# Attention in 64x64 quadrants of TensorE on blocks of 256 rows, two rows on a partition, with a planner that orders the jobs of all engines

## The chip, the cores and the metric

One core of one Trainium2 chip. The metric is the device time of one execution in microseconds (us); a kernel is run several times in turn with the kernel before on the same chip, and the median and the range are given. A run is called slow when it is over 1.5% above the fastest run of the same kernel, otherwise fast; ratios use fast runs only. Engines: PE is TensorE (PEld its weight loads), DVE is VectorE, ACT is ScalarE, POOL is GpSimd, SP is SyncE, whose queue issues nearly all transfers here.

## The reference

A retention layer (attention without a softmax, with a decay between positions) and then a gated MLP. Eight sequences of 576 rows, 8 heads of 64, all inputs fp32.

```python
scores = scale * np.matmul(q, k.transpose(0, 1, 3, 2))
gamma = 1.0 - 2.0 ** (-5.0 - np.arange(H))
Dmat = np.where(rel >= 0, gamma[:, None, None] ** rel[None], 0.0)   # rel = row - column
x = np.matmul(scores * Dmat, v)                 # heads side by side: [8, 576, 512]
h = gelu_tanh(x @ w_in)                         # [.., 1024]
u, v = h[..., :512], h[..., 512:]
v_n = (v - mean) / sqrt(var + 1e-6) * g_ln
v_s = np.einsum('ts,bsd->btd', w_sg, v_n) + b_sg[None, :, None]   # mixes the 576 rows of a sequence
out = x + (u * v_s) @ w_out
```

Since the decay is a product of a factor of the row and one of the column, the kernel multiplies q and v by powers of gamma, works in blocks of rows, and carries the sum of k times v of earlier blocks as a state.

## The kernel before

Two sequences make 9 tiles of 128 rows. A tile is loaded with one row on a partition, so that each contiguous run of a transfer is 64 fp32 values, 256 bytes. Attention uses the whole array for the transposes, half of its rows for the scores, half of its columns for the tile's own part of the output, and the whole array, with a block-diagonal state that is half zeros, for the state's part.

```python
def load(i):
    ...
            nc.sync.dma_start(t[p0:p0 + n, :, :], src[2 * p + b, :, r0:r0 + n, :].transpose([1, 0, 2]))

def attn_T(i):      # 8 transposes of 128x128
    ...
            nc.tensor.transpose(tp[:, a, kk, :], f[:, a, kk * 128:(kk + 1) * 128], ident[:])

def attn_S(i):      # 8 matmuls on half of the rows
    ...
            nc.tensor.matmul(sc[:, hh, kk, :], s["qkT"][r, 1, kk, :], s["qkT"][r, 0, kk, :], ...)

def attn_O(i, evac):
    ...
            nc.tensor.matmul(ot[:, kk, :n], st["zbd"][:, kk, :], s["qkT"][:, 0, kk, :n], ...)      # state
    ...
            nc.tensor.matmul(ot[64 * hh:64 * hh + 64, kk, :], s["vb"][:, 2 * kk + hh, :], s["ret"][:, hh, kk, :], ...)
```

The weights: w_in is loaded in quarters, each one transfer over 128 partitions, `moe_w_in.rearrange("(c p) f -> p c f", p=128)`. The order of everything is written out in one loop over the tiles, which also deals out units of gating (`mlp_W`) and final projection (`mlp_O`) between the attention steps. Gating mixes all rows of a sequence, so none can start before the first 576 rows, w_sg and its transposes are through.

## Time and profile before

| | before |
|---|---|
| median of 4 runs | 249.22 us (249.12 to 250.46) |
| profiled span | 248.1 us |
| TensorE busy | 220.2 us, 89% |
| packets under 512 bytes | 113,824 of 120,606 |

A table of stretches of the kernel before. The columns are: the stretch in us, its length, busy us (and instructions) of PE, PEld, DVE, ACT and POOL, the granted TensorE clock, the mean busy share of the DMA engines, and GB/s.

```profile
0.00:20.00 20.00, 12.98 (x133) 6.46 (x134) 16.95 (x37) 5.97 (x9) 11.49 (x26) 0.93 1.03 235
20.00:60.00 40.00, 32.25 (x397) 24.39 (x401) 22.77 (x40) 23.75 (x44) 25.13 (x41) 0.91 0.96 197
140.00:220.00 80.00, 76.17 (x906) 53.74 (x919) 46.33 (x77) 50.28 (x95) 49.20 (x81) 1.00 0.73 163
```

Up to 60 us the DMA engines are full (shares of 1.03 and 0.96) and TensorE has holes; from 140 on TensorE is busy 95% and the DMA engines 73%.

Busy time hides how much of TensorE is really used, because matmuls overlap in the pipeline: in this kernel a 128-column matmul is shown as 219 ns and the next one starts 56 ns after it. So I use one more measure below, **lost TensorE time** up to a moment. Every matmul group has a weight load in the trace, and those records are complete (144 loads for the gating input `hv`, of whose 144 matmuls the trace before holds 126). I give each the step at which its matmuls follow one another when nothing holds them (the steps of the prediction: 216 ns for 512 columns, 122 for 288, 56 for 128 and half of that for half of the array; for quadrants 8 for 64 columns, 14 for 128, and 16 in the state update, where I take two to run together; 0 for filler matmuls), sum the steps of all loads issued by that moment, and subtract the sum from the moment. It contains idle time, fillers, changes of the array's shape, drains, and time at a lower granted clock. The 14 and the 16 are estimates, a quarter of 56 and twice 8. In the changed kernel forty quadrant matmuls of 128 columns start within 123.79 to 124.38 us, 15 ns each, and the sixteen of a state update take 120.85 - 120.49 = 0.36 us with a change of shape of 0.10 behind them, 16 ns each. The absolute value leans on these steps; differences between kernels with the same matmuls don't. The clock's part is at most the length of a stretch times what the granted clock lacks to 1: by 60 us up to 5.0 us in the kernel before (0.93 and 0.91 in the table), 1.6 in the changed kernel, 3.6 in its second trace. So differences of 2 or 3 us in the lost time of two traces can be the clock's.

### The profile page before, as it was taken

The page shows a single profiled execution, that of the slowest core. Times are in us where ns is not written, and L with a number is a line of the kernel's source. Part 1 is how long each engine was busy: PE and PEld are TensorE (multiplying, and loading weights), DVE is VectorE, ACT ScalarE, POOL GpSimd, SP SyncE. Part 2 cuts the span into 40 slices and gives each one's busy share as a digit, 9 for nine tenths or more (in the row PEclk, how much of TensorE's full clock was granted, in tenths as well). Part 3 has the DMA queues.
Part 4 walks back from the last instruction along what each step waited for, and adds up shares of the span by engine and source line. Part 5 has one row for each costly group of instructions (what it writes and reads, how often), then busy time and mean ns, then how long its engine had stood idle before and what let it go on. Part 6 is the DMA issues. An engine that isn't in the chain of part 4 may idle for free.

```text
span 248.1 us, 6439 instructions
## 1 busy us (share of the span) xinstructions
PE 220.2 (89%) x2543; PEld 154.0 (62%) x2580; DVE 141.4 (57%) x251; ACT 141.7 (57%) x258; POOL 137.3 (55%) x237
## 2 busy tenths in 40 slices
PE   7737749889998999989998999899989999899893
PEld 2415547677655776666666776577657766676561
DVE  8984636747645665556646764476537554564240
ACT  2334566844665656756574667756565657755512
POOL 4387948652674776656655656555646766441100
PEclk9988997979999999999999999999999999999999
DMA  7999999693677985892898965993879778201314
GB/s 151 284 281 221 225 239 232 142 189 68 142 177 203 206 174 122 234 230 49 186 229 182 215 151 152 223 203 81 193 199 211 167 171 184 74 3 42 128 45 169
DMA packets 120606, 42.02 MB, mean 169 GB/s; under 512 B 113824, under 2 KB 114424, under 8 KB 120576
## 3 DMA queue, kind: packets, MB, share of 16 engines
q1 hardware_dynamic: 119376, 40.93, 72.7%
q0 software_dynamic: 656, 0.66, 1.7%
q8 instruction: 20, 0.33, 0.6%
q10 hardware_dynamic: 544, 0.02, 0.1%
q14 instruction: 10, 0.08, 0.1%
HBM read 32.80 MB, written 9.44 MB: 170 GB/s over the span
## 4 chain that ended last, share of the span: by engine, by line
PE 71%; POOL 4%; ACT 3%; issue 3%; DVE 2%; DMA 1%; ACTq 0%; POOLq 0%; DVEq 0%
PE wp L339 14%; PE hu L327 11%; PE op L355 11%; PE hv L289 11%; PE tp L221 6%; PE ot L254 4%; PE sc L233 3%; PE op L352 3%; PE zp L275 3%; PE ot L250 2%; ACT vn L317 1%; POOL qkb L200 1%; POOL vb L200 1%; PE wtp L192 1%; ACT vmid L314 1%
## 5 line engine op out<-in xcount | busy, mean ns | idle before, releaser
L237 DVE TENSOR_TENSOR ret<-sc,tri 128x1024 bf16<-128x1024 f32 x32 | 39.0, 1220 | 28.3 <-PE sc L233 28.3
L343 DVE TENSOR_TENSOR gT<-wp,uT 128x288 bf16<-128x288 f32 x64 | 29.3, 457 | 41.8 <-PE wp L339 41.7
L302 POOL TENSOR_SCALAR rs<-mv 128x1 f32<-128x1 f32 x36 | 8.0, 223 | 78.9 <-DVE mv L300 50.4
L339 PE MATMUL wp<-wT,vn 128*128 128x288 bf16 x256 | 42.7, 289 | 3.7 <-ACT vn L317 3.7
L200 POOL TENSOR_TENSOR qkb<-qf,gqv 128x512 bf16<-128x512 f32 x36 | 37.6, 1044 | 5.1 <-DMA qf<-in_q_dram 4.9
L292 ACT ACTIVATE vg<-hv 128x512 f32<-128x512 f32 x36 | 21.5, 597 | 32.5 <-issue 18.4
L327 PE MATMUL hu<-xT,w_in 128*128 128x128 bf16 x576 | 39.4, 223 | 0.0
L200 POOL TENSOR_TENSOR vb<-vf,gqv 128x512 bf16<-128x512 f32 x36 | 37.4, 1038 | 3.5 <-DMA vf<-in_v_dram 3.5
L330 ACT ACTIVATE uT<-hu 128x512 bf16<-128x512 f32 x36 | 21.5, 597 | 28.6 <-PE hu L327 28.6
L289 PE MATMUL hv<-w_in,xT 128*128 128x512 bf16 x126 | 36.4, 390 | 1.5 <-issue 0.6
L327 PEld LDWEIGHTS <-w_in 128*128 128x128 bf16 x576 | 35.0, 100 | 0.3
L355 PE MATMUL op<-w_out,gT 128*128 128x512 bf16 x126 | 33.1, 379 | 0.9
L339 PEld LDWEIGHTS <-vn 128*128 128x128 bf16 x256 | 24.3, 98 | 12.7 <-ACT vn L317 5.0
L358 ACT ACTIVATE ob<-op 128x512 f32<-128x512 f32 x36 | 21.4, 594 | 18.8 <-PE op L355 18.5
L298 DVE BATCH_NORM_STATS2 bst<-vg 128x6 f32<-128x512 f32 x36 | 24.8, 688 | 11.9 <-ACT vg L292 11.9
L223 DVE COPY qkT<-tp 128x1024 bf16<-128x1024 bf16 x36 | 24.1, 669 | 7.7 <-PE tp L221 7.7
L221 PE MATMUL tp<-ident,qkb 128*128 128x128 bf16 x288 | 23.8, 227 | 3.4 <-POOL qkb L200 2.5
L258 ACT ACTIVATE xT<-ot 128x512 bf16<-128x512 f32 x36 | 21.2, 590 | 8.6 <-PE ot L254 8.1
L317 ACT ACTIVATE vn<-vg,nm,rs 128x512 bf16<-128x512 f32 x32 | 25.8, 805 | 0.1
L221 PEld LDWEIGHTS <-qkb 128*128 128x128 bf16 x288 | 17.1, 101 | 8.3 <-POOL qkb L200 3.4
L339 PE MATMUL wp<-wT,vmid 128*128 128x288 bf16 x64 | 18.5, 289 | 4.2 <-ACT vmid L314 2.7
L303 POOL TENSOR_TENSOR rs<-rs,mhalf 128x1 f32<-128x1 f32 x36 | 20.4, 567 | 3.0
(72 smaller groups left out, 275.3 us busy)
## 6 DMA issues: line engine op xcount, KB each, us to landing
out_dram<-ob SPq DMA_DIRECT2D x36, 256.0 KB, 2.2
qf<-in_q_dram SPq DMA_DIRECT2D x32, 256.0 KB, 4.1
kf<-in_k_dram SPq DMA_DIRECT2D x32, 256.0 KB, 4.7
vf<-in_v_dram SPq DMA_DIRECT2D x32, 256.0 KB, 4.7
wst<-in_moe_w_in_dram SPq DMA_DIRECT2D x4, 512.0 KB, 5.5
qf<-in_q_dram SPq DMA_DIRECT2D x8, 128.0 KB, 3.3
kf<-in_k_dram SPq DMA_DIRECT2D x8, 128.0 KB, 3.4
vf<-in_v_dram SPq DMA_DIRECT2D x8, 128.0 KB
```

Source lines behind the costliest of these rows:

```text
L200: nc.gpsimd.tensor_tensor(out_[:], in_[:], gqv[:, a, m, :].unsqueeze(2).to_broadcast([128, H, D]), op=Alu.mult)
L221: nc.tensor.transpose(tp[:, a, kk, :], f[:, a, kk * 128:(kk + 1) * 128], ident[:])
L223: nc.vector.tensor_copy(qkT[:], tp[:])
L237: nc.vector.tensor_tensor(ret[:].rearrange("p a k t -> p (a k) t"), sc[:].rearrange("p a k t -> p (a k) t"), msk[:].unsqueeze(1).to_broadc ...
L289: nc.tensor.matmul(hv[:], xTs[p][:, kk, 128 * m:128 * m + 128], w_in[:, kk, F2:], start=(kk == 0), stop=(kk == KK - 1))
L292: nc.scalar.activation(vg[:], hv[:], Act.Gelu_apprx_tanh)
L298: nc.vector.bn_stats(bst[:], vg[:])
L317: nc.scalar.activation(vn[:], vg[:], Act.Identity, scale=rs[:], bias=nm[:])
L327: nc.tensor.matmul(hu[:, c, :], w_in[:, kk, 128 * c:128 * c + 128], xTs[p][:, kk, 128 * m:128 * m + 128], start=(kk == 0), stop=(kk == KK ...
L339: nc.tensor.matmul(ps[:], vns[t0 + j][e][:, 128 * c:128 * c + 128], wT[e][j][:, half * HS:(half + 1) * HS], start=(j == 0), stop=(j == SB ...
L343: nc.vector.tensor_tensor(gTs[p][:, c, col:col + HS], ps[:], uTs[p][:, c, col:col + HS], op=Alu.mult)
L355: nc.tensor.matmul(op[:], gTs[p][:, c, r], w_out[:, c, :], start=False, stop=(c == KK - 1), skip_group_check=True)
```

## The change

The intent: TensorE bounds the kernel, so attention goes to 64x64 quadrants, four matmuls at a time, without the half-empty state. Blocks grow to 256 rows with two neighbouring rows on a partition, so the runs of a transfer are 512 bytes. The handwritten order is replaced by a planner that, while the program is built, simulates all engines with assumed durations and lays down the order in which each engine's jobs then run. Its assumptions for a transfer are in `place`. The diff, cut to its core:

```diff
+class Planner:
+    def place(self, j, t):
+        j.start = t
+        if j.nbytes:
+            self.free[j.eng] = t + j.dur
+            per = (8.0 + 0.0325 * j.run) * j.nbytes / j.run / 16.0
+            self.dma_free = max(self.dma_free, t + 1300.0) + per + 100.0
+            j.out = self.dma_free + 700.0
+            self.dmas.append(j.out)
...
-    def load(i):
-                nc.sync.dma_start(t[p0:p0 + n, :, :], src[2 * p + b, :, r0:r0 + n, :].transpose([1, 0, 2]))
+    def a_load(b, t):
+        f_ = new("ld", [128, H, 2 * D], F32)
+        if ns == 2:
+            nc.sync.dma_start(f_[:], src[2 * p + e, :, r0:r0 + 256, :].rearrange("h (p s) d -> p h (s d)", s=2))
+        else:      # the 64 rows at the end of one sequence and the 64 at the start of the next
+            for c, (e, r0) in enumerate(ch):
+                nc.sync.dma_start(f_[64 * c:64 * c + 64, :, :D], src[2 * p + e, :, r0:r0 + 64, :].rearrange("h p d -> p h d"))
...
-            nc.sync.dma_start(wst[:], moe_w_in.rearrange("(c p) f -> p c f", p=128)[:, c:c + 2, half * F2:(half + 1) * F2])
+            w4 = moe_w_in.rearrange("(a c h d) f -> a c d h f", a=2, c=2, h=2)
+            for cc in range(2):
+                nc.sync.dma_start(wst[half, c][64 * cc:64 * cc + 64], w4[c, cc, :, :, half * F2:(half + 1) * F2])
...
+    def a_T(b):
+                            R, C = slice(64 * r, 64 * r + 64), slice(64 * c, 64 * c + 64)
+                            nc.tensor.transpose(tpf[C, r, o:o + 64], qkb[R, s, a, 2 * kk + c, :], ident[R, R])
...
+    def a_OS(b, g):              # output of block b, with the last scores of block b + 1 in it
+        a_O(b, st.pop((b, "zs")))
+        a_S(b + 1, g)            # (not for the first two blocks and the last one)
+        nc.tensor.drain()
+        a_O2(b)                  # the half of the state part whose quadrants write the other bank
...
+    FREE = 1                     # up to this block the scores stay outside the output step
+    pl.plan()
```

The MLP's matmuls are the same; only their order is the planner's.

## The prediction

> **What bounds the kernel now.** I read the page first, then the groups, the timeline of one steady block, and last a table of stretches.
>
> ```profile
> PE 220.2 (89%) x2543; PEld 154.0 (62%) x2580; DVE 141.4 (57%) x251; ACT 141.7 (57%) x258; POOL 137.3 (55%) x237
> ...
> PE   7737749889998999989998999899989999899893
> ...
> PEclk9988997979999999999999999999999999999999
> DMA  7999999693677985892898965993879778201314
> ```
>
> TensorE (PE) is the busiest engine by far; the others are near 57%. The first nine slices (6.2 us each) look different from the rest: PE has holes while DMA stands at 9. So there are two regimes. The starts of the score matmuls (line 233) bound the stretches of the next table: the first scores start at 8.43 us, those of block 7 at 56.81, those of the last block at 223.50. Its columns are length, busy us (and count) of PE, PEld, DVE, ACT and POOL, granted clock, DMA share, GB/s.
>
> ```profile
> 0.00:8.43 8.43, 6.40 (x37) 2.88 (x38) 7.17 (x24) 2.23 (x3) 3.69 (x13) 1.00 0.84 205
> 8.43:56.81 48.38, 35.69 (x454) 25.82 (x461) 29.79 (x49) 25.93 (x46) 32.92 (x53) 0.89 1.05 219
> 56.81:223.50 166.69, 158.58 (x1883) 112.37 (x1911) 97.02 (x164) 103.25 (x192) 98.60 (x165) 1.00 0.73 164
> 223.50:248.10 24.60, 19.58 (x173) 12.90 (x174) 7.44 (x15) 10.23 (x17) 2.08 (x6) 1.00 0.25 97
> ```
>
> In the head the DMA engines are full (1.05) and the clock drops to 0.89; in the long middle PE is busy 158.6 of 166.7 us at full clock. Busy is not throughput, so I took steps from one start to the next:
>
> ```profile
> 119.06 0.62 PE L221 MATMUL tp<-ident,qkb 128*128 128x128 bf16 x8
> 119.52 1.06 PE L327 MATMUL hu<-xT,w_in 128*128 128x128 bf16 x16
> 120.41 0.65 PE L339 MATMUL wp<-wT,vn 128*128 128x288 bf16 x4
> 120.90 0.29 PE L339 MATMUL wp<-wT,vmid 128*128 128x288 bf16 x1
> 121.02 0.39 PE L352 MATMUL op<-ident,xT 128*128 128x128 bf16 x4
> 121.46 0.81 PE L355 MATMUL op<-w_out,gT 128*128 128x512 bf16 x3
> 122.21 0.40 PE L233 MATMUL sc<-qkT 64*128 64x128 bf16 x8
> 122.54 1.04 PE L289 MATMUL hv<-w_in,xT 128*128 128x512 bf16 x4
> ```
>
> The first column is the start. Sixteen 128-column matmuls take 120.41-119.52 = 0.89 us, 56 ns each; the five of 288 columns take 122 ns each. A 512-column one steps by 216 ns in the single records. Eight half-array score matmuls run in pairs, 4 x 56 = 0.22 us, yet the next full-array one starts 0.33 us after them: changing the array's shape costs about 0.1 us (93 ns in the records). The kernel's own warm-up already has quadrant matmuls (64 x 64 weights, 64 columns):
>
> ```profile
> 8.76 0.45 PE L409 MATMUL scr<-warm 64*64 64x64 bf16 x32
> ```
>
> One lasts 193 ns, so the last starts at about 9.01: 31 steps in 0.25 us, 8 ns each, four in 32 ns.
>
> By these steps, with counts from the program (some records are missing in the trace), PE's work is 190 us: MLP and its weights 144.2, attention 46.0 (transposes 288 x 56 = 16.1; scores 288 x 28 = 8.0; state part of the output 6.8; own part 288 x 28 = 8.0; state update 128 x 56 = 7.1). With 4 shape changes per 128-row block, 144 x 0.093 = 13.4. What is left of the span is idle: 8.4 before the first scores, 20 in blocks 0 to 6, 10 in the 28 blocks of the middle (0.35 each), 5 in the last stretch, and 2 of filler matmuls. The middle is bound by PE's issue, the head by loads.
>
> [...] The changed kernel does that with a drain and a semaphore in every output step. The old kernel has no such step, so its trace can't price it.
> - [...] a 128-column matmul is shown as 219 ns but steps by 56.
> - [...] The page has 113,824 of 120,606 packets under 512 B; the median record of a 256 B packet is 18 ns, of a 2048 B one 84 ns.
>
> **The change part by part.** I counted instructions in the compiled order of both kernels.
> - *Transposes:* 288 full ones become 1152 of 64x64. 1152 x 7.9 ns = 9.1 us against 16.1: -7.0.
> - *Scores:* 512 x 128 columns and 64 x 64 columns in quadrants: 512 x 14 + 64 x 7.9 = 7.7 against 8.0: -0.4. Mask and chunk stay at 128 rows.
> - *State update:* 480 of 64 columns, but a chunk's rows lie in one half of the array, so only two run together: 480 x 15.8 = 7.6 against 7.1: +0.4.
> - *Output, both parts:* 224+512 of 128 columns and 32+64 of 64: 736 x 14 + 96 x 7.9 = 11.0 against 14.8: -3.8. The old one multiplied by a block-diagonal state that was half zeros.
> - Attention sum: 35.4 against 46.0, **-10.7 us**.
> - *Shape changes:* the order has 106 against 145: 39 x 0.093 = **-3.6**.
> - *Drain:* 20 output steps wait for the scores ahead of them to leave the array. A matmul shows 0.22 us and steps by 0.056, so an estimate is 0.2 us each: **+4**.
> - *Loads:* two rows on a partition make runs of 512 B. Interpolating between 18 and 84 ns gives some 27 ns per 512 B packet, an estimate, so 299 against 227 GB/s. By 57 us some 9.4 MB of q, k, v are loaded: 31.5 instead of 41.5 us of a full queue, **-10** in the head. In the middle loads are hidden either way.
> - *First block:* twice as big, and POOL now also casts k that ACT cast before; its first scores come later, by some 2 us of the same head: **+2**, partly covered by the planner's first-projection-before-second-block order.
> - *Order:* PE jobs are chosen by earliest start and due time; in the middle I give it a third of the 10 us: **-3**. The tail is the same chain (last projection, statistics, norm, gating, output): 0. Fillers run in gaps: 67 instead of 18, nothing on the path. The MLP has the same matmuls.
> - VectorE copies the same transpose and mask volume in bigger pieces, ScalarE evacuates the same xT and state; both fall or stay, about 140 us of work each, so neither binds at 220.
>
> Sum: -10.7-3.6+4-10+2-3 = -21. With rounding to whole stalls that I can't place, 249 - 21 = 228, or counted forward: 179.5 (work) + 9.9 (106 changes) + 4 + 18 (head) + 7 + 5 + 1 (time over span) = 224. I take the forward sum, because the order of the head is new as a whole.
>
> **Rivals.**
> 1. *Evacuation becomes the wait.* Transposes, scores and output now share two PSUM buffers of two banks each, and a copy of 2048 transposed elements takes twice the 669 ns of now. For: every output step needs both buffers free at once. Against: a 256-row block holds them for some 8 us of 2 x 10.5. If it bites, 0.5 us for each of 20 blocks: 234.
> 2. *A plan that the chip doesn't keep.* The order is fixed from assumed durations; each engine runs strictly in that order, so one late job holds those behind it. For: the head depends on landings, which the trace shows at 4 to 5.5 us with wide variation. Against: POOL, DVE and ACT have 40% slack. It would cost 5 to 15 us: up to 240.
> 3. *The planner is much better than I allow.* If head stalls fall to 10 and middle stalls to 3, 211.
> 4. *Loads were hidden anyway.* Then the head's holes are dependences (fewer matmuls exist before the first gating) and the 10 us don't come: 234. The two in 8.43:56.81 can't be told apart without a run.
>
> **Range and chances.** 224 us; a range of 211 to 238 holds rivals 3 and 1 or 4. To stay within 2% (above 244), the drain and the plan must eat the whole saving in matmuls and loads; I give that 0.06, and slower 0.03.
>
> **What would show it.** Right: transposes stepping by 8 ns; a score group to a projection about 0.1 us beyond its own steps; q, k, v packets of 512 B near 27 ns; block 3's scores (row 640 on) before 40 us; a steady 256-row block in 10.4 to 10.8 us against 11.9 now. Wrong: quadrant steps above 12 ns, PE waiting for VectorE or ScalarE in most blocks, a drain of over 0.5 us, or PE idle in the head as now.

## The result, and the profile after

| | before | after |
|---|---|---|
| median | 249.22 us | 241.47 us (239.23 to 242.31, 4 runs) |
| profiled span | 248.1 us | 239.6 us |
| ratio | | 0.968 (95% interval 0.961 to 0.975) |
| the same kernel again (e1) | 249.00 us | 239.78 us, ratio 0.965 (0.958 to 0.971) |

A ratio is the mean time of one kernel's fast runs over that of the other's in the same rounds, so it is not quite the ratio of the medians. The change is faster by 3.2% by the ratio. I had predicted 224 us with a range of 211 to 238: the direction was right, the size was less than half of what I said, and 241.5 is outside the range.

The page of the changed kernel: busy engines, slices of 6 us each, packets, and the chain that ended last.

```profile
PE 215.4 (90%) x4440; PEld 148.0 (62%) x4485; DVE 137.1 (57%) x230; ACT 135.1 (56%) x234; POOL 126.8 (53%) x198
...
PE   7975839887989999999999999899999999999993
...
DMA  6999589999899985898564658971110220111324
GB/s 177 251 237 259 138 260 328 290 277 267 176 302 280 310 219 149 244 294 238 149 196 137 193 140 253 298 198 47 48 47 11 80 94 34 59 47 44 131 92 175
DMA packets 70765, 42.92 MB, mean 179 GB/s; under 512 B 14817, under 2 KB 63993, under 8 KB 70721
...
PE 76%; DMA 13%; issue 4%; ACT 3%; SPq 1%; POOL 1%; ACTq 0%
```

The packets are indeed bigger. From slice 11 on TensorE is at 9 nearly throughout. But the first ten slices have holes as before, and 13% of the chain that ended last is DMA, against 1% before. The same stretches as above:

```profile
0.00:20.00 20.00, 17.22 (x219) 8.26 (x223) 16.93 (x31) 4.62 (x7) 14.07 (x31) 1.00 0.99 230
20.00:60.00 40.00, 28.96 (x730) 20.39 (x737) 20.43 (x33) 23.27 (x41) 26.75 (x35) 0.96 0.96 258
140.00:220.00 80.00, 76.89 (x1588) 54.19 (x1602) 45.19 (x75) 50.38 (x89) 34.69 (x57) 1.00 0.34 104
```

The 17.22 us of PE in the first 20 are mostly fillers (55 of the head's 67, 12 us by their steps). Between 20 and 60 us TensorE is busy less than before, 29.0 against 32.3 us, although the transfers move 258 instead of 197 GB/s. In the lost TensorE time:

| lost TensorE time, us | before | after | after, second trace (e1) | predicted for after |
|---|---|---|---|---|
| 0 to 20 us | 17.1 | 18.1 | 18.1 | |
| 20 to 60 us | 15.0 | 19.1 | 18.5 | |
| together, up to 60 us | 32.1 | 37.2 | 36.6 | about 21 |
| 60 us to the end | 25.1 | 22.3 | 20.3 | about 22.5 |
| work by the steps | 190.8 | 180.1 | 180.1 | 179.5 |

The column "predicted" comes from the prediction's forward sum: 18 for the head, and of its 9.9 + 4 for shape changes and drains those that fall before 60 us (26 of 106 changes in the trace, 2.4 us, and some 5 drains, 1 us); the rest of its 44.9 us belongs after 60, less the 1 us by which a time exceeds the profiled span. The work is no test of the prediction, since it is the same counts with the same steps; that the part after 60 us came out as predicted is one. So **the whole miss of 16 to 17 us lies before 60 us**. The clock doesn't explain it: the changed kernel had the higher granted clock there (1.00 and 0.96 against 0.93 and 0.91).

Its single steps can be read from a steady stretch of the changed kernel (start, duration to the last end, engine, line, operation, count):

```profile
119.75 0.29 PE L575 MATMUL wp<-wT,vmid 128*128 128x288 bf16 x1
119.97 0.71 PE L367 MATMUL pp<-ident,qkb 64*64 64x64 bf16 x64
120.49 0.42 PE L421 MATMUL zp<-vb,qkb 64*64 64x64 bf16 x16
...
124.38 0.39 PE L393 MATMUL pp<-qkT 64*64 64x128 bf16 x12
124.88 0.24 PE L439 MATMUL pp<-qkT,zb 64*64 64x128 bf16 x2
```

The 64 quadrant transposes take 120.49 - 119.97 = 0.52 us, 8 ns each. The change of shape ahead of them is 119.97 - 119.75 - 0.12 = 0.10 us. The drain shows in the last two lines: the twelve scores need about 12 x 14 = 0.17 us, so the last starts near 124.55, and the held-back part of the output starts at 124.88: 0.3 us where I had put 0.2. The other output steps with scores in them from 60 to 205 us show the same, 0.31 to 0.33 us. All of that is close to the prediction.

What TensorE waits for in the head is found with the other engines. The waits of the changed kernel between 20 and 62 us (engine and line, what ended the wait, us in total, times, longest):

```profile
POOL qkb L350 <- DMA ld<-in_q_dram: 12.9, 3, 5.7
...
ACT wnat L295 <- DMA ld<-in_moe_w_sg_dram: 5.5, 2, 4.8
...
PE zp L421 <- ACT zb L427: 4.4, 2, 4.1
```

GpSimd, which scales q, waits three times for q to land, 12.9 us in all. ScalarE waits 4.8 us for w_sg, and behind it in its queue stands the eviction of the state for which TensorE then waits 4.1 us. The landings in the trace (some of them read from the instruction that waited for the data) against those that the plan assumes, in us: q of block 1 20.8 against 13.9, v of block 2 31 against 20.8, first part of w_sg 32.8 against 21.6, q of block 3 38 against 26, q of block 4 46.8 against 33.6. By packets, 9.42 MB had been moved by 40 us in the kernel before, and 9.23 MB in the changed one: **in the first 40 us the bigger packets brought no byte earlier.** By 60 us it is 12.65 against 14.95 MB. One gap stands out, from 24 to 30 us, just after SyncE has issued the four small transfers into the middle tile's buffers (21.7 to 24.4 us); the columns are those of the stretches above:

```profile
24.00:30.00 6.00, 5.25 (x195) 4.16 (x196) 4.21 (x5) 1.58 (x3) 3.66 (x4) 1.00 0.59 141
```

### The profile page after: what moved, and what is told of

The parts are those of the page before. It is cut to its first block, busy times and chain, and to the rows that moved or that the text cites. A ratio compares the mean times of both kernels' runs of the same rounds, so it can differ in the third digit from the quotient of the medians.

```text
span 239.6 us, 10051 instructions
## 1 busy us (share of the span) xinstructions
PE 215.4 (90%) x4440; PEld 148.0 (62%) x4485; DVE 137.1 (57%) x230; ACT 135.1 (56%) x234; POOL 126.8 (53%) x198
## 4 chain that ended last, share of the span: by engine, by line
PE 76%; DMA 13%; issue 4%; ACT 3%; SPq 1%; POOL 1%; ACTq 0%
PE wp L575 17%; PE hu L559 13%; PE op L596 13%; PE hv L517 12%; PE pp L439 7%; DMA ld<-in_q_dram 4%; PE pp L367 4%; PE pp L393 4%; PE op L593 3%; DMA ld<-in_moe_w_out_dram 3%; DMA ld<-in_moe_w_in_dram 3%; PE zp L421 3%; DMA ld<-in_moe_w_sg_dram 2%; ACT xT L506 1%; PE scr L248 1%
## 5 line engine op out<-in xcount | busy, mean ns | idle before, releaser
L403 DVE TENSOR_TENSOR ret<-pp,msk 128x1024 bf16<-128x1024 f32 x32 | 38.9, 1220 | 27.8 <-PE pp L393 27.6
L350 POOL TENSOR_TENSOR qkb<-ld,gqv 128x512 bf16<-128x512 f32 x36 | 37.1, 1051 | 15.6 <-DMA ld<-in_q_dram 12.9
L350 POOL TENSOR_TENSOR vb<-ld,gqv 128x512 bf16<-128x512 f32 x36 | 38.2, 1081 | 5.8 <-DMA ld<-in_v_dram 3.6
L582 DVE TENSOR_TENSOR gT<-wp,uT 128x288 bf16<-128x288 f32 x64 | 28.7, 453 | 21.0 <-PE wp L575 20.8
L521 ACT ACTIVATE vg<-hv 128x512 f32<-128x512 f32 x36 | 21.5, 596 | 20.3 <-PE hv L517 18.1
L372 DVE COPY qkT<-pp 128x2048 bf16<-128x2048 bf16 (+1 forms) x20 | 22.2, 1111 | 15.1 <-PE pp L367 15.1
L548 ACT ACTIVATE vn<-vg,mv 128x512 bf16<-128x512 f32 x32 | 25.0, 809 | 8.8 <-POOL mv L536 8.7
L506 ACT ACTIVATE xT<-pp 128x512 bf16<-128x512 f32 (+1 forms) x40 | 24.6, 665 | 8.2 <-PE pp L439 8.2
L575 PEld LDWEIGHTS <-vn 128*128 128x128 bf16 x256 | 23.9, 98 | 6.7
L517 PEld LDWEIGHTS <-xT 128*128 128x128 bf16 x144 | 12.6, 98 | 13.1 <-ACT xT L506 2.4
L341 POOL CAST qkb<-ld 128x1024 bf16<-128x1024 f32 (+1 forms) x20 | 19.5, 975 | 0.5 <-DMA ld<-in_k_dram 0.5
L248 PE MATMUL scr<-warm 128*128 128x512 bf16 x61 | 17.6, 436 | 2.2 <-DVE warm L221 1.2
L421 PE MATMUL zp<-vb,qkb 64*64 64x64 bf16 x480 | 13.8, 194 | 6.1 <-ACT zb L427 4.4
```

Of the source, the lines that this page charges most:

```text
L350: nc.gpsimd.tensor_tensor(dst[:, s], src[:, s], gqv[:, a, 2 * n + s, :].unsqueeze(2).to_broadcast([128, H, D]), op=Alu.mult)
L372: nc.vector.tensor_copy(st[b, "qkT"][:].rearrange("p c a k t -> p c (a k t)")[:, :, :w], st.pop((b, "tp"))[:].rearrange("p c a k s t -> p ...
L403: nc.vector.tensor_tensor(ret[:].rearrange("p r (k t) -> p (r k) t", k=2), sc[:].rearrange("p r (k t) -> p (r k) t", k=2), msk2[:].rearran ...
L506: nc.scalar.activation(dst, src, Act.Copy)
L517: nc.tensor.matmul(hv[:], xTs[p][:, kk, 128 * m:128 * m + 128], w_in[:, kk, F2:], start=(kk == 0), stop=(kk == KK - 1))
L521: nc.scalar.activation(vgs[i][:], cur.pop(("hv", i))[:], Act.Gelu_apprx_tanh)
```

## The experiments

Eighteen kernels ran, in five groups, each group on one chip with its own runs of the kernel before. The rivals for the lost head: A, the loads of w_in, now in halves of 64 partitions, are slow; B, the order is wrong because the plan's landings are; C, the bytes of q, k and v bound the head, whatever the order; D, the fused output step holds block 2 until block 3 has landed. E and F came later: queue order of one tile, and a late start of block 0.

### Which term is it

**e1, the unaltered kernel again.**

> The changed kernel unaltered, as the base on this chip: some 241.5 us, ratio to the kernel before 0.968. All theories say the same; it sets the base for the other three.

239.78 us (238.71 to 241.66), ratio 0.965. The same within the spread of this kernel, about 3 us, which is larger than that of the kernel before. Differences below 2 us are therefore read from the lost time or left open.

**e2, w_in in full-width loads.**

```diff
-            for cc in range(2):
-                nc.sync.dma_start(wst[half, c][64 * cc:64 * cc + 64], w4[c, cc, :, :, half * F2:(half + 1) * F2])
+            for hh in range(2):
+                nc.sync.dma_start(wst[half, c][:, hh, :], w4[c, :, :, hh, half * F2:(half + 1) * F2])
```

> The eight loads of the first weight matrix each fill all 128 partitions (one row of 512 columns) in place of 64 partitions with two rows; same bytes, packets, number and order. Theory A (half-partition weight loads are slow: their 2048 B packets take 144 ns against 84 in the kernel before, 1024 packets x 60 ns / 16 = 4 us of the full queue in the first 20 us): packets back to 85 to 95 ns, second block's q lands 3 to 4 us earlier, time 236 to 239. Rival (the first 20 us are bound by the memory's rate, some 250 GB/s, whatever the shape): packets of q and k get slower in exchange and the time stays within 1 us of the base.

271.06 us, ratio 1.090. A failed experiment, with something to learn. The slices of e2, 6.7 us each:

```profile
DMA  7311114659999899997985654799111012112224
GB/s 182 100 51 51 51 51 119 184 129 297 330 276 277 211 261 274 305 277 201 315 229 152 184 160 143 198 267 303 70 43 42 34 49 81 45 42 78 96 104 157
```

For four slices only 51 GB/s arrive at a DMA share of 0.1. From 10 to 36 us the queue of w_in took 13.1% of the time of the 16 engines, which is the time of 2.1 engines, an estimate by this share. Why this form of the load fills no more, no run shows. What e2 shows about the question is only this: 17.6 us more lost by 60 us became 29.6 us in the time (271.06 - 241.47), since the delay went on (25.1 us more lost by 100 us; the granted clock was 0.50 from 20 to 60 us, which is part of it). Here a late head was not made up later.

**e3, the plan with slower transfers.**

```diff
-            per = (8.0 + 0.0325 * j.run) * j.nbytes / j.run / 16.0
+            per = 1.4 * (8.0 + 0.0325 * j.run) * j.nbytes / j.run / 16.0
```

> Only the planner's own estimate of a transfer is multiplied by 1.4, so that its landings agree with the measured ones (second block's q 18.3 us in the plan against 20.8 measured; 13.9 in the plan as it was). Theory B (the order of ScalarE and TensorE in the head is made for landings that come 7 to 13 us too early, so jobs that are ready sit behind casts of weights that have not landed: ScalarE 27.9 to 32.8 us, TensorE 4.1 us behind it): the 4.1 us wait of the state update goes, 3 to 7 us gained, 235 to 238. Rival (TensorE would find nothing else to do, loads bound the head): less than 1.5 us.

242.98 us (241.35 to 243.87), ratio 0.975; lost by 60 us 39.5. A plan nearer to the real landings is not better, if anything worse (0.969 to 0.980 against 0.958 to 0.971 for e1). B in this plain form falls.

**e4, half of q, k and v (wrong result on purpose, relative error 1.27).** Four of eight heads are loaded and used twice; all compute instructions stay, and read the four heads twice.

```diff
-            nc.sync.dma_start(f_[:], src[2 * p + e, :, r0:r0 + 256, :].rearrange("h (p s) d -> p h (s d)", s=2))
+            nc.sync.dma_start(f_[:, :4], src[2 * p + e, :4, r0:r0 + 256, :].rearrange("h (p s) d -> p h (s d)", s=2))
...
```

> Wrong result on purpose: of q, k, v only four of eight heads are loaded and used twice, so half the bytes and packets of these loads with the same order, instructions and packet sizes. If loads bound the head (theory C), the 30 us of queue time of q, k, v in the first 60 us fall to 15 and the time falls by 8 to 14 us, to 228 to 234. If the head is bound by dependences, by the order or by issue of transfers, by less than 3 us.

229.00 us (228.69 to 229.48), ratio 0.921 (0.918 to 0.924): 10.8 us below e1 of the same chip. Its stretches:

```profile
0.00:20.00 20.00, 17.24 (x221) 8.18 (x224) 16.33 (x31) 5.20 (x8) 16.06 (x35) 1.00 0.88 193
20.00:60.00 40.00, 36.07 (x963) 26.30 (x972) 27.55 (x44) 29.18 (x51) 31.41 (x48) 1.00 0.69 191
```

TensorE's first 20 us stay as they were; between 20 and 60 TensorE is busy 36.1 instead of 29.0 us, while the DMA share falls to 0.69. Lost time by 60 us: 29.3 against 36.6. C is supported: half of the bytes of q, k and v cost 10.8 us, 7.3 of them in the head and some 3.5 later. Of the 7.3, up to 3.6 show up as granted clock (1.00 in e4, 0.91 between 20 and 60 us in e1). But 29 us stay lost even so, 18 of them before 20 us. The weights were loaded whole in e4, so it doesn't say what those are made of.

### The form of the loads

**e5, both halves of w_in in flight at once** (the upper halves from ScalarE's queue).

```diff
-            for cc in range(2):
-                nc.sync.dma_start(wst[half, c][64 * cc:64 * cc + 64], ...)
+            for cc, q_ in enumerate((nc.sync, nc.scalar)):
+                q_.dma_start(wst[half, c][64 * cc:64 * cc + 64], ...)
```

> The half-partition loads of the first weight matrix stay as they are, but the lower halves are issued by SyncE and the upper halves by ScalarE, so that both halves are in flight at once (the run with one row per load gave two-engine transfers and told nothing of this). Theory A (144 ns a packet comes from filling only 64 partitions at a time): packets fall to 84 to 100 ns, the weights land by 14 us in place of 17, and the time falls by 2 to 4 us from the base of 239.8. Rival (it comes from the source, or from the mixture with 512 B packets): packets stay over 130 ns, time within 1 us of the base.

240.61 us, ratio 0.965, packets still 150 ns (median of the 2048-byte packets): no help. ScalarE's four issues took until 14.5 us, and the last packet of w_in began at 21.6 us, so the time is no clean test of the form; the length of the packets is.

**e7, runs of 256 bytes again.**

```diff
-            nc.sync.dma_start(f_[:], src[...].rearrange("h (p s) d -> p h (s d)", s=2))
+            for s_ in range(2):
+                nc.sync.dma_start(f_[:, :, s_ * D:(s_ + 1) * D],
+                                  src[...].rearrange("h (p s) d -> p s h d", s=2)[:, s_])
```

> Undoes one part: every q, k, v load of a 256-row block is two transfers of 256 B runs (one per row slot) in place of one of 512 B runs; same tiles, same order. By the step of the prediction (512 B runs gave 10 us in the head) this should cost 8 to 12 us: 248 to 252, with first gating at 69 or later. Rival (the head's rate is some 250 GB/s with either, as the kernel before reached 280 to 290 GB/s with 256 B runs beside full-width weights): 1 to 4 us.

258.35 us, ratio 1.036 (1.033 to 1.039): the bigger runs are worth some 17 to 19 us in this kernel. But not where I had put them. By 60 us e7 has lost 41.6 against 37.2, only 4.4 us more; 12.7 are lost between 100 and 140 us, where the changed kernel loses 3.9 (up to 5.2 of the 12.7 can be the granted clock, 0.87 there). That stretch of e7, and its two waits that matter:

```profile
100.00:140.00 40.00, 31.67 (x651) 22.52 (x653) 18.24 (x30) 19.13 (x33) 15.53 (x24) 0.87 0.99 238
```
```profile
ACT ob L602 <- DMA out_dram<-ob: 10.4, 2, 6.3
...
PE hu L561 <- ACT ob L602: 5.9, 1, 5.9
```

The DMA engines are full there (a share of 0.99), the output stores come late, their buffers stay taken, ScalarE waits 10.4 us for one, and TensorE for ScalarE. The same stretch of the changed kernel has a DMA share of 0.67. The experiment doubles the number of transfers too, so it overstates the price of the runs alone.

**e8, block 1 loaded between the two halves of w_in.**

```diff
-    ju = [win_load(0, 0), win_load(0, 1)]
     loads(1)
+    ju = [win_load(0, 0), win_load(0, 1)]
```

> Order of loads as in the kernel before: second half of the first weight matrix, block 1, the other half, block 2 (the changed kernel loads both halves first). Theory C (loads bound the head, so what is needed later should land later): block 1's v lands 4 us earlier but the halves later; first gating within 2 us of 60.6, time 238 to 240. A gain of over 3 us would say that the order of loads, not their sum, set the head.

240.66 us (238.49 to 242.16), ratio 0.963; lost by 60 us 35.9. This other order of the loads makes no difference that the runs can tell.

**e12, w_in in the old form (wrong result on purpose, relative error 0.44)**: one transfer of 128 partitions a quarter, rows permuted.

```diff
-            for cc in range(2):
-                nc.sync.dma_start(wst[half, c][64 * cc:64 * cc + 64], w4[c, cc, :, :, half * F2:(half + 1) * F2])
+            nc.sync.dma_start(wst[half, c][:], moe_w_in.rearrange("(c p) f -> p c f", p=128)[:, 2 * c:2 * c + 2, half * F2:(half + 1) * F2])
```

> Wrong on purpose: each quarter of w_in comes in one transfer over all 128 partitions, as in the kernel before, so its rows are permuted and the MLP's result is wrong; the times stay comparable. Theory A2 (the two half-partition transfers with a head-interleaved source make the 2048-byte packets slow): their packets fall from 144 ns to 84 to 95 ns, w_in has landed near 14 us instead of 17.1, the first gating comes about 3 us earlier and the time is near 237 us. If the mixing with 512-byte packets makes them slow, they stay near 140 ns and the time at 239 to 242 us.

**e13, halves of 64 partitions, but with the plain order of rows (wrong on purpose).**

```diff
+            ws = moe_w_in.rearrange("(c p) f -> p c f", p=128)
             for cc in range(2):
-                nc.sync.dma_start(wst[half, c][64 * cc:64 * cc + 64], w4[c, cc, :, :, half * F2:(half + 1) * F2])
+                nc.sync.dma_start(wst[half, c][64 * cc:64 * cc + 64], ws[64 * cc:64 * cc + 64, 2 * c:2 * c + 2, half * F2:(half + 1) * F2])
```

> Wrong on purpose: each quarter of w_in still comes in two transfers of 64 partitions, but with the plain order of rows of the kernel before (rows p and 128+p on a partition) instead of rows d and 64+d. If the half-partition form makes the 2048-byte packets slow, they stay near 144 ns, w_in lands near 17 us and the time is 239 to 242 us. If the order of the source's rows does, they fall to about 88 ns, w_in lands near 14 us and the time is 235 to 238 us.

The transfers between 6 and 18 us, first of the changed kernel, then of e12, then of e13 (the engines are full in all three: the queue of these transfers shows 110 to 112% of the time of the 16 engines):

```profile
DMA packets 2917, 2.93 MB, mean 244 GB/s; under 512 B 265, under 2 KB 1893, under 8 KB 2917
```
```profile
DMA packets 4897, 3.98 MB, mean 331 GB/s; under 512 B 234, under 2 KB 3872, under 8 KB 4896
```
```profile
DMA packets 2909, 2.88 MB, mean 240 GB/s; under 512 B 353, under 2 KB 1885, under 8 KB 2909
```

The 2048-byte packets of w_in took 145, 88 and 152 ns (medians), and the last of them began at 17.0, 13.8 and 17.2 us. So it is the 64 partitions and not the order of rows; with e5, packets don't get shorter when the other half is in flight (150 ns). The stretch moved 244 and 240 GB/s with the halves, 331 with loads over all partitions. What makes 64 partitions slower, no run shows. I had not priced it, though the diff shows the 64 in plain sight. In the time e12 has 236.27 us (234.71 to 237.89), ratio 0.946 (0.939 to 0.952), some 5 us below the changed kernel by its median; e13 has 239.92 us, ratio 0.962 (0.957 to 0.967), no different from it. Lost by 60 us: 34.0 and 37.4; moved by 40 us: 10.58 and 9.40 MB.

### The order of the head

**e6, FREE = 5** (the first six blocks keep their scores outside the output step).

```diff
-    FREE = 1
+    FREE = 5
```

> In the first six blocks the output step is no longer fused with the next block's second score step (one constant: FREE = 5 in place of 1). Theory D (in the head a block's output, and so all its MLP work, is held until the next block has landed and been transposed: output of block 2 at 44.3 us though its own scores left at 36.6): block 2's output moves to 38 to 40 us, the first gating matmul from 60.6 to 54 to 57 us, time 235 to 237. Rival (loads bound the head, the order only moves idle time about): within 1.5 us of 239.8.

239.55 us (235.63 to 241.16); one fast run at 235.63 and three that count as slow against it, so there is no ratio. Output of block 2 came at 40.6 instead of 44.4 us, the first gating product at 59.4 instead of 60.6 (e1). The lost time by 60 us is 34.7, some 2 us less, but in the trace of the one fast run. D is left open: the runs neither show a gain nor exclude one of 2 us.

**e9, the middle tile first.**

```diff
...
+    for jl in (J["v", 4], J["q", 5], J["k", 5]):
+        jl.deps.append(J["rs", 2])
+    J["x", 3, 0].deps.append(J["n", 4])
     pl.plan()
```

> Four lines are added ahead of the plan: GpSimd may prepare v of block 4 and q and k of block 5 only after the small norm steps of the middle tile, and ScalarE evicts block 3's output only after it has normalised that tile. Loads, tiles and instructions stay the same; only the order of GpSimd and ScalarE changes. In the changed kernel the middle tile's statistics were ready about 51 us, GpSimd took its norm steps at 55.6 us behind 4 us of preparations, and the first gating product came at 61.3 us (60.6 in the second run). Theory E (queue order: the late loads made the planned order of the in-order engines wrong for this tile): first gating near 54 to 55 us and a time of 234 to 237 us, if what is put off does not come back. Theory C alone (loads): the work put off returns as a new wait, first gating moves under 2 us, time 239 to 242.

GpSimd in the changed kernel, and then in e9 (start, duration):

```profile
54.47 1.04 POOL L350 TENSOR_TENSOR qkb<-ld,gqv 128x512 bf16<-128x512 f32 x1
55.60 0.23 POOL L533 TENSOR_SCALAR mv<-mv 128x1 f32<-128x1 f32 x1
```
```profile
52.93 0.23 POOL L533 TENSOR_SCALAR mv<-mv 128x1 f32<-128x1 f32 x1 [0.66 <-DVE mv L529]
...
54.38 2.04 POOL L350 TENSOR_TENSOR vb<-ld,gqv 128x512 bf16<-128x512 f32 x2
```

The edit did what it was to do: the middle tile's small steps now wait for VectorE alone and come 2.7 us earlier, and the first gating product comes at 58.8 instead of 61.3 us. The time stays: 241.04 us, ratio 0.967, lost by 60 us 38.8. What was gained there was lost again elsewhere; I did not follow where. E falls in this form.

**e10, e9 with FREE = 5.**

```diff
+    # the four lines of e9
-    FREE = 1
+    FREE = 5
```

> The same four lines, and FREE = 5, so that the first blocks' outputs don't wait for the next block's scores. FREE = 5 alone brought the output of block 2 from 44.4 to 40.6 us, but the first gating only from 60.6 to 59.4 us. If that gain was swallowed by the order of GpSimd (theory E), the two edits add up to more than their sum: first gating near 50 to 52 us, time 229 to 233 us. If the loads alone set the first gating, it stays above 57 us and the time at 237 us or more.

First gating product at 57.3, time 240.09 us, ratio 0.963, lost by 60 us 35.8. Also no gain that the runs can tell from e1. The moment of the first gating product, which I had used as a gauge up to here, is not one: e11 below has it at 63.8 us and is faster.

**e11, the zeroing of the middle tile's buffers after block 0, and the small transfers into them after w_out.**

```diff
+    j_zero.deps.append(J["v", 0])
+    j_pv.deps.append(wo[1][0])
     pl.plan()
```

> Two lines: the zeroing of the middle tile's buffers goes after GpSimd's work on block 0, and the small transfers into them after the second half of w_out has landed. GpSimd ran 3.5 us of zeroing before q of block 0, which had landed at 4.2 us, and the small transfers sat in a stretch in which the DMA share fell to 0.57. Theory F (late start of block 0 and the gap in issuing): the first scores come about 3 us earlier, v of block 3 lands 2 to 3 us earlier, first gating 58 to 59 us, time 237 to 239 us. If w_in's landing bounds the first V product (17 us, V at 20.7 us), the earlier scores change nothing: time 239 to 242 us.

GpSimd at the start, in the changed kernel and in e11:

```profile
7.55 0.52 POOL L630 MEMSET vmid<- 64x512 bf16 x1
8.13 2.29 POOL L350 TENSOR_TENSOR qkb<-ld,gqv 128x512 bf16<-128x512 f32 x2
```
```profile
5.35 2.04 POOL L350 TENSOR_TENSOR qkb<-ld,gqv 128x512 bf16<-128x512 f32 x2 [1.49 <-DMA ld<-in_q_dram]
```

238.67 us (237.80 to 243.81), ratio 0.956 (0.951 to 0.962) against 0.965 and 0.968 of the changed kernel: about 2.5 us, with intervals that still touch. Transposes of block 0 come 3 us earlier (8.9 us), but its first scores only at 15.3 us as before (15.5), behind the casts of w_in and the row preparations on VectorE. So the gain, if it is one, does not come from an earlier start. Without the gap in which SyncE issued the four small transfers, 10.33 instead of 9.23 MB are moved by 40 us, which fits; the lost time by 60 us is 35.0, but the granted clock was 1.00 in this trace, so most of these 2 us can be the clock's.

### Putting the parts together

**e14, a correct kernel with full-width loads of w_in.** The old transfers, and four casts of 64 partitions a quarter, two of which move their half to the other 64 partitions. The plan's durations of the casts were raised with it.

```diff
+            for hh in range(2):
+                for cc in range(2):
+                    i = src[64 * hh:64 * hh + 64, cc, :]
+                    o = w_in[64 * cc:64 * cc + 64, 2 * c + hh, half * F2:(half + 1) * F2]
+                    if eng == "DVE":
                        nc.vector.tensor_copy(o, i)
                    else:
                        nc.scalar.activation(o, i, Act.Copy)
...
```

> Correct: w_in comes in one transfer a quarter over all 128 partitions in the old order, and the casts to bf16, now four of 64 partitions each, put the halves where the new layout wants them. Packets near 88 ns as in the wrong version; the casts take about twice as long (some 1.4 us a quarter on VectorE and 2 us on ScalarE). If the landing of w_in was worth 5 us: time 236 to 238 us. If the longer casts eat it: 239 to 242 us.

243.54 us, ratio 0.976 (0.971 to 0.982): if anything slower than the changed kernel (0.971 is the upper end of e1's interval), although its packets take 88 ns and 10.56 MB are moved by 40 us. VectorE in e14:

```profile
13.95 4.97 DVE L281 CAST w_in<-ld 64x512 bf16<-64x512 f32 x8
18.95 1.23 DVE L373 COPY qkT<-pp 128x2048 bf16<-128x2048 bf16 x1
```

Eight casts take 5.0 us (0.41 to 1.18 us each), and the eviction of block 0's transposes stands behind them. The first V product comes at 28.0 instead of 20.7 us.

**e15, e14 with e11 and FREE = 5**

```diff
+    # the edits of e6, e11 and e14 together
```

> Correct: the loads of w_in of e14, the later zeroing of e11 and FREE = 5 together. If the three took separate shares of the time lost in the head (about 4, 3 and 2 us): lost TensorE time by 60 us falls from 37 to about 29 us and the time to 231 to 234 us. If they remove the same wait, the best of them alone sets it: 236 to 238 us.

243.02 us (238.25 to 245.49); of six runs four count as slow; fast runs: ratio 0.959 (0.952 to 0.967).

**e16, e14 with e11**

```diff
+    # the edits of e11 and e14 together
```

> Correct: e14 and e11 together, FREE left at 1. Separate shares: 232 to 235 us, lost TensorE time by 60 us about 31 us. The same wait: 236 to 238 us. Against e15 it prices FREE = 5 once the loads come earlier: at most 2 us.

243.93 us (238.97 to 244.49); three of four runs slow, no ratio. Both of e15 and e16 carry the eight casts of e14 (first V product at 27.8 and 28.0 us), both profiles fell into slow runs, and neither is a gain that I can show.

**e17, e16 with VectorE freed for block 0.**

```diff
+    j_rows.deps.append(J["Se", 1, 1])
+    ju[0][1].deps.append(J["Se", 0, 1])
+    ju[1][1].deps.append(J["x", 0, 1])
```

> Correct: e16's kernel, with VectorE freed for block 0: the casts of the second half of w_in come after block 0's scores (ScalarE's after block 0's output), the small row preparations after block 1's scores. If e14 lost its gain to VectorE's order, the first V product comes at 18 to 19 us (20.7 in the changed kernel), lost TensorE time by 60 us is 31 to 33 us and the time 234 to 237 us. If the time lost in the head has another bound (the loads of blocks 1 to 5 behind w_in), it stays at 238 us or more.

239.05 us (236.66 to 241.47; four fast runs), ratio 0.953 (0.947 to 0.959): the best of the correct kernels, some 1.3% below the changed one by the ratios; its interval lies just below that of the changed kernel's first measurement and touches that of e1. The first V product comes at 18.7 instead of 20.7 us. The lost time by 60 us is 35.2, but this profile, too, fell into a slow run (241.33 us), with a granted clock of 0.94 up to 60 us, which is up to 3.6 us; so it can't be set against e11.

**e18, the same order with the loads of w_in as in the changed kernel.**

> Correct: e11's kernel with the same order of VectorE and ScalarE, and the loads of w_in as in the changed kernel. If the loads' width matters: 1 to 3 us slower than e17. If only the order does: the same as e17 within 1 us. Against e11 (238.7 us): 0 to 2 us faster.

239.46 us (238.16 to 240.66), ratio 0.959 (0.955 to 0.964). First V product at 18.8 us as well, lost by 60 us 35.4. So the earlier V came from the order of VectorE, and the full-width load adds less than the runs can tell in a correct kernel (the two intervals overlap, on one chip). What may count next is block 1, whose transposes begin at 22.6 (e17) and 23.9 us (e18) against 24.0 in the changed kernel; no run tests that.

## Why the prediction was wrong

**Right, by its own steps.** The work by the steps fell by 10.7 us, which follows from the counts; what the traces show is that the steps hold: 8 ns a quadrant transpose, and in the steady stretch little beyond the steps but shape changes and drains. The shape changes are 106, as counted, at 0.10 us in the timeline. The drain is about 0.3 us where I had 0.2: some 2 us over 20 blocks. VectorE and ScalarE did not become the bound (57% and 56% busy), and from 60 us on the list of waits has TensorE's matmuls wait 0.3 us for ScalarE and never for VectorE, so rival 1 is out. After 60 us 22.3 us were lost where the forward sum had about 22.5.

**The step that failed** is the head in the forward sum, "18 (head)", and in it the line "Loads: ... **-10** in the head". Some 34 us were lost there besides shape changes and drains (37.2 - 2.4 - 1), where I had 18, and this is the whole miss of 16 to 17 us. The head before had 28 by the prediction's own count (8.4 + 20), so it did not become 10 us better but some 5 worse. Two slips in the sum are small beside that: 18 is 8.4 + 20 - 10 and leaves out the "+2" for the first block, and of the 9.4 MB of q, k and v only 8.4 had come in 256-byte packets by 57 us. The runs put three things in its place:

1. The head did not get its bytes faster until 40 us. I took 299 GB/s for all that comes before 57 us. The 512-byte packets do take 27 ns as estimated (the median over the trace). But by 40 us 9.23 MB had been moved, 9.42 before; only between 40 and 60 us was it more, 5.7 against 3.2 MB. Undoing the runs (e7) cost only 4.4 us by 60 us. What they gained up to 40 us was spent again by w_in in halves (145 ns for 2048 bytes instead of 84 to 88) and by a gap in issuing (141 GB/s at a share of 0.59 from 24 to 30 us). Where one of the two is mended, 10.3 to 10.6 MB are moved by 40 us (e11, e12, e14). I had priced neither, though both are in the diff and in the compiled order. By the times, the halves cost 4 us (e12 against e13, ratios 0.946 and 0.962) and the gap perhaps 2.5 (e11).
2. The bytes of q, k and v still bound the head from 20 to 60 us: half of them take 10.8 us off the time and 7.3 off the lost time by 60 us (e4). Rival 4 (loads hidden, holes are dependences) had the outcome right, since the 10 us did not come, but not the reason: e4 shows that the loads are not hidden. What the 29 us are that stay with half the loads, no run shows.
3. The 18 us were already gone at 20 us, before the first V product; that much was lost before, too (17.1). Between 20 and 60 us blocks land one by one, and the first gating product comes only at 61.3 us. My 18 had no room for that second stretch: 19.1 us are lost there, against 15.0 before.

**The other rivals.** Rival 2 (a plan that the chip does not keep) describes what is seen, since landings come up to 13 us after the planned ones; but neither a plan with slower transfers (e3) nor the right order for the tile that was held up (e9) gained anything that the runs can tell. So the late data is the better account of its 5 to 15 us; that a third order would gain is not excluded, since changes of order do move the time by 1% (e17, e18). I had also written "In the middle loads are hidden either way": e7 shows that this holds for the 512-byte runs and not for 256-byte runs in this order (12.7 us lost between 100 and 140 us).

**A sign that I gave and that failed:** block 3's scores before 40 us. They came at 44.6 and 47.2. A steady pair of sequences took 50.1 and 50.8 us between equal transposes (69.84 to 119.97 and on to 170.78), 11.1 to 11.3 us for 256 rows against 11.9 before; I had 10.4 to 10.8. The lost time after 60 us shows no excess, because this sign was stricter than the forward sum: its terms for the steady part give (179.5 + 9.9 + 4 + 7) / 18 = 11.1 us for 256 rows, which is what came. The prediction also says that every output step has "a drain and a semaphore"; the program has the drain alone, since the mark for the semaphore is dropped before it is used.

**What stays open.** The contributions do not add up. Full-width loads in the wrong kernel, later zeroing and halved bytes each lower the lost time by 60 us (by 2 to 3, 2 and 7 us; for the last two, part of it can be the clock, as said above), but the correct kernels with two or three of the edits stay at 35 us or more. Of those only e18's trace is of a fast run. And earlier bytes alone are not enough: e14, in a fast run, had moved 1.3 MB more by 40 us than the changed kernel and is not faster. How much of the 29 us left with half the loads could be filled, with gating started at 40 us for instance, no run shows.

## What to carry to other kernels

When a change mixes instructions, loads and order, cost each by stretch: here the instruction terms held to a microsecond or two, and the error was in the head: a credit of 10 us for its loads, in a stretch in which several things share the queue, became a loss of 5. Before crediting a faster transfer, add up which bytes have to be in by when, by the form of every transfer in the stretch (how many partitions: 145 against 88 ns a packet here; what share of the engines it fills: 13% in e2; how often issued: 141 GB/s in the gap), and not only that of the tensors that the change is about. And gauge the head by lost work, not by one event: the first gating product came earlier or later without the time following it. Look at the granted clock and the state of the traced run before comparing the lost time of two traces.

## What the traces and runs priced

- A change of the array's shape was 0.10 us in the timeline of the changed kernel. An explicit drain between two quadrant groups cost about 0.3 us.
- 64 quadrant transposes of 64 columns took 0.52 us in the changed kernel: 8 ns each, 32 ns for a set of four.
- In these traces a 512-byte packet took 27 ns (median), 2048 bytes 84 to 88 ns over all partitions: by the byte, 512-byte packets reach some 80% of the rate of 2048-byte ones. Between 6 and 18 us, beside w_in's halves, they took 35 ns (median).
- Over 64 partitions the 2048-byte packets of w_in took 145 to 152 ns; the stretch with w_in's halves and other packets moved 240 to 244 GB/s, and the rate of the halves alone was not measured here.
- The load over all partitions had its price in the longer casts that then put its halves in place: eight casts of 64 partitions and 512 elements took 5.0 us in all on VectorE (e14), where two of 128 partitions and 1024 elements took 0.67 us each in e12.
